# Score and maximum pairs in groups of six, pv halves in threes

## The chip, the cores and the metric

The kernel runs on one core of one Trainium2 chip. The metric is the device time of one execution in microseconds, as the median over runs. The core's engines are named as in the profile: PE is TensorE (PEld its weight loads), DVE is VectorE, ACT is ScalarE, POOL is GpSimd, and SP issues transfers. Each engine works through its own queue in order; semaphores make one engine wait for another.

## The reference

A transformer block with modulation by a condition vector `c`, over 2048 rows of 512: softmax attention with 32 heads of 16, then a gated feed-forward layer of width 1792.

```python
def _A_ref(x, wqkv, wo):
    B, S, D = x.shape
    H = 32; Dh = D // H
    qkv = (lambda x, *d: x.transpose(*d))((x @ wqkv).reshape(B, S, 3, H, Dh), 2, 0, 3, 1, 4)
    q, k, v = qkv[0], qkv[1], qkv[2]
    scale = Dh ** -0.5
    scores = jnp.einsum("bhqd,bhkd->bhqk", q, k) * scale
    p = _softmax(scores, axis=-1)
    o = jnp.einsum("bhqk,bhkd->bhqd", p, v)
    return (lambda x, *d: x.transpose(*d))(o, 0, 2, 1, 3).reshape(B, S, D) @ wo

def _B_ref(x, w_gate, w_up, w_down):
    g = _silu(x @ w_gate)
    u = x @ w_up
    return (g * u) @ w_down
...
h = _layernorm(x, axis=-1) * (1 + ca) + sa
x = x + ga * _A_ref(h, A_wqkv, A_wo)
h = _layernorm(x, axis=-1) * (1 + cb) + sb
x = x + gb * _B_ref(h, B_w_gate, B_w_up, B_w_down)
```

All of it is in float32; where the kernel uses the faster fp32r type, it splits a number into a high and a low part.

## The kernel before

**Stages.** First the normalised rows are projected to q, k and v. Then attention runs. While it runs, the feed-forward layer of the first three of four chunks of 512 rows is worked into it; the last chunk comes behind it.

**Attention.** A unit is one chunk of 512 queries and one group of four heads; there are 32 units of 16 steps, one step for each 128 keys, so n = 512 steps. A step has four scores, one for each head, and two pv halves. Three things run at different places of the sequence:

- `max_one` (L470): a matmul of 128 queries by 512 keys (L479) into one of the banks of the turn `four`, and a maximum over the keys on DVE (L481). It runs LEAD = 21 steps ahead of the scores, because a softmax needs the row maxima before its exps. Four of them belong to each step.
- `max_rows` (L483): once for a unit, when its maxima are complete, the row maxima are reduced (L486), negated (L498), turned into rows by PE (L491 to L493, in a bank from the turn `bank`), copied by ACT (L495) and stored beside q (L497), so that the score matmul subtracts them. It is appended to the list `side`, whose entries are run one after each pair: the turning is the fifth entry.
- `score` (L500): a matmul of 128 keys by 512 queries (L506) into a bank of the turn `bank`, and the exp on ACT into a tile `pt_` (L508). There are PTS = 13 such tiles.
- `pv_step` (L510): one half of 256 queries: four matmuls, one for each head, each onto 32 rows of the unit's own bank 7 (L521). In the profile a half shows as two passes of four. A step's four `pt_` tiles come free with its second half. After the last step of a unit ACT copies the bank out (L525).

A pair (`pair_of`, L903) is one score and one `max_one`. The order of the heads is chosen so that the two matmuls lie on opposite halves of the rows of PE, and the profile shows them side by side.

**The order of PE** is written by hand. `pvs(most, by_halves)` (L914) issues up to `most` pv halves of steps whose scores are all at least four pairs back; with `by_halves` it stops at the end of a unit and owes what is left to the next call. There are two kinds of stretches:

- `plain(steps, tails)` (L936): attention alone. `four` turns over banks 0 to 3, `bank` over banks 4, 5 and 6. It works in windows of WIN = 3 pairs, each followed by one or two pv halves (HALVES = 2, 1, 1, 2). With `tails`, transposes for the feed-forward layer come behind the last windows.
- `filled(places, work)` (L949): eight pairs with feed-forward matmuls between them, then up to six pv halves.

`end_steps` (L930) calls `after(i)` for steps that are done, which issues the loads and stores that have come due and the calls of `max_rows`.

**Where `plain` is called.** Once with 147 steps before any feed-forward work; then for each of the first three chunks with 9 steps, and with 3 steps with tails; with 3 steps ahead of the last two `down` jobs of the first two chunks; with 21 steps between chunks, twice; and with 24 steps (REST) in the third chunk. The calls without tails are nine, with 147, 9, 3, 21, 9, 3, 21, 9 and 24 steps.

Of the kernel before, what the change touches and what calls it, by code (L numbers as in the profile page):

```python
# [39 lines left out]
WIN = 3  # L40
HALVES = (2, 1, 1, 2)
# [60 lines left out]
def block_kernel(ctx, tc, x, wqkv, wo, w_gate, w_up, w_down, c, w_mod, out):  # L102
# [19 lines left out]
    four, bank, single = Turn(0, 1, 2, 3), Turn(4, 5, 6), Turn(7)  # L122
# [387 lines left out]
    def pv_step(i, half):  # L510

        u, kt = divmod(i, 16)
        g = u % NG
        cols = slice(half * HQ, (half + 1) * HQ)
        if kt == 0 and half == 0:
            pv[u] = single("pv")
            o_[u] = pf.tile([P, CW], F32, name="o", tag="o", bufs=2)
        p_ = pts.pop(i) if half else pts[i]
        for h in range(4):
            e0 = (kt * H + 4 * g + h) * (DH + 1)  # L520
            nc.tensor.matmul(pv[u][32 * h:32 * h + 32, cols], v_flat[:, e0:e0 + 32], p_[h][:, cols],  # L521
                             start=(kt == 0 and half == 0), stop=(kt == 15),
                             skip_group_check=half == 1)
        if kt == 15 and half:
            nc.scalar.copy(o_[u], pv[u])  # L525
# [318 lines left out]
    def close_unit(u, i):  # L844

        if u == NU - 1:
            res[u] = out_a(u, nc.scalar)
            return
        res[u] = out_a(u, nc.sync)
        if u + 3 < NU:  # L850
            load_k(u + 3)
            load_q(u + 3)
        i0 = i if u % NG == NG - 1 else i + 2
        at(i0 + 3, lambda: res.__setitem__(u, out_b(u, nc.sync, *res[u])))
        at(i0 + 4, lambda: res.__setitem__(u, out_r(u, nc.sync, *res[u])))
        at(i0 + 5, lambda: out_c(u, nc.gpsimd, nc.gpsimd, *res.pop(u)))
        if u % NG == NG - 1:
            if u // NG:
                at(i + 4, lambda: begin(u // NG))
                at(i + 5, lambda: chunks[u // NG].load_wo())  # L860
            at(i + 7, lambda: chunks[u // NG].load_o(nc.gpsimd))
            at(i + 9, lambda: chunks[u // NG].split_o())
# [37 lines left out]
    done, ended, owed = 0, 0, 0  # L900
    three = Turn(0, 1, 2)

    def pair_of():  # L903
        nonlocal done
        i = done // 4 - 1
        most = 4 * n - 4 * (LEAD - 1)
        score(i + 1, (ORDER if done < most else (0, 1, 2, 3))[done % 4])
        if done < most:
            max_one(done + 4 * (LEAD - 1))
        done += 1  # L910
        if side:
            side.pop(0)()

    def pvs(most, by_halves):  # L914

        nonlocal owed
        if by_halves:
            most, owed = most + owed, 0
        while most and halves and 4 * halves[0][0] + 8 <= done:
            i, half = halves.pop(0)  # L920
            pv_step(i, half)
            most -= 1
            if i % 16 == 15 and half:
                close_unit(i // 16, done // 4 - 1)
                if by_halves:
                    break
        if by_halves and most and halves and 4 * halves[0][0] + 8 <= done:
            owed = most

    def end_steps():  # L930
        nonlocal ended
        while ended < done // 4:
            after(ended - 1)
            ended += 1

    def plain(steps, tails=()):  # L936

        nonlocal four, bank
        assert steps % WIN == 0 and done % 4 == 0
        four, bank = Turn(0, 1, 2, 3), Turn(4, 5, 6)  # L940
        for w in range(4 * steps // WIN):
            for _ in range(WIN):
                pair_of()
            if w >= 4 * steps // WIN - len(tails):
                tails[w - 4 * steps // WIN](four())
            pvs((HALVES[(w - 2) % 4] if done > 8 else 0) + (w == 4 * steps // WIN - 1), True)
            end_steps()

    def filled(places, work):  # L949
# [25 lines left out]
    for ci in range(last):  # L975
        plain(STARTS[ci] - done // 4)
        ch = chunks[ci]
        for t0 in (0, 2):
            work = out_pair(ch, t0, outs, True)
            filled(TWO, work)  # L980
            filled(TWO, work)
        side.append(lambda: scaled(ch))
        plain(NORM)
        plain(WIN, [lambda tp, k=k: ch.turned(tp, k) for k in range(NK)])
        if ci == last - 1:
            plain(REST)
        for _ in range(len(ch.jobs) - (KEEP if ci == last - 1 else 0)):
            job, args = ch.jobs.pop(0)
            if args == (NF // FG - 1, 0):
                plain(WIN)  # L990
            work = job(ch, *args, outs, True)
            for places in (TWO, TWO) if job is gate_up else (DOWN,):
                filled(places, work)
# [73 lines left out]
```

## Time and profile before

| | |
|---|---|
| median of 3 runs | 1879.55 us |
| lowest and highest run | 1879.51 and 1881.34 us |
| span of the profiled execution, first to last instruction | 1875.6 us |
| PE busy in it | 1846.7 us |
| DVE busy in it | 1541.8 us |
| ACT busy in it | 1252.4 us |

The page gives no other time for the profiled execution than its span, so sums are made against the span, and the 3.95 us between span and median are carried along. Engines overlap: their busy times add up to more than the span. A line such as `L506 PE MATMUL bank<-qop,kop` names the line of the kernel, the engine, the operation, and what is written from what. In a listing in order of time the first number is the start and the second the duration, both in us; the part in square brackets is the idle time before it and what ended it. A matmul counts as busy from its start until its last result is written, so that PE looks full when matmuls follow each other without overlapping fully.

### The profile page before, as it was taken

What the parts mean: (1) busy time and instruction counts of PE and PEld (TensorE: products, weight loads), DVE (VectorE), ACT (ScalarE), POOL (GpSimd) and SP (SyncE); (2) the same over time, 40 slices, a digit from 0 to 9 for tenths busy, and PEclk for the clock granted to TensorE, in tenths of its full rate; (3) what the DMA queues carried; (4) which work ended last, traced back from release to release, by engine and by line L of the source; (5) the groups of instructions that cost most, each with busy time, mean ns of one, the idle gap of its engine ahead of it and who ended that gap; (6) DMA issues with size and microseconds to landing.
All of it is one profiled execution on the core that took longest, in us unless ns stands there. A gap on an engine that the chain in (4) does not pass through costs nothing.

```text
span 1875.6 us, 41002 instructions
## 1 busy us (share of the span) xinstructions
PE 1846.7 (98%) x16996; PEld 1160.4 (62%) x16996; DVE 1541.8 (82%) x2558; ACT 1252.4 (67%) x2406; POOL 415.3 (22%) x498
## 2 busy tenths in 40 slices
PE   7999999999999999999999999999999999999999
PEld 5766444444455766666555667666554566667887
DVE  5548999999999888888999888889999988831643
ACT  4221888888887766777777776677878877674211
POOL 3000454456323211111133111111123011030200
PEclk9999999999999999999999999999999999999999
DMA  8855677766843534554454454453643446243642
GB/s 286 292 198 142 174 183 178 201 167 190 211 86 78 145 102 124 144 124 90 107 124 116 108 127 131 121 122 78 159 86 56 108 92 156 86 159 119 249 180 110
DMA packets 78854, 267.62 MB, mean 143 GB/s; under 512 B 17364, under 2 KB 22484, under 8 KB 57988
## 3 DMA queue, kind: packets, MB, share of 16 engines
q1 hardware_dynamic: 59820, 180.10, 33.0%
q0 software_dynamic: 18160, 84.10, 19.0%
q8 instruction: 133, 2.18, 0.5%
q10 hardware_dynamic: 688, 0.80, 0.1%
q14 instruction: 53, 0.43, 0.1%
HBM read 201.85 MB, written 62.13 MB: 141 GB/s over the span
## 4 chain that ended last, share of the span: by engine, by line
PE 95%; DVE 2%; ACT 2%; DMA 0%; issue 0%; SPq 0%; ACTq 0%; DVEq 0%
PE bank L521 26%; PE bank L506 22%; PE bank L719 19%; PE bank L479 10%; PE bank L729 7%; PE bank L209 7%; DVE mx L481 1%; PE bank L762 1%; PE bank L491 1%; PE bank L162 0%; PE bank L703 0%; DMA wm_ab<-in_w_mod 0%; DVE stt L745 0%; PE bank L279 0%; PE bank L493 0%; PE bank L492 0%
## 5 line engine op out<-in xcount | busy, mean ns | idle before, releaser
L481 DVE TENSOR_REDUCE mx<-bank 128x1 f32<-128x512 f32 x2048 | 1286.5, 682 | 119.5 <-PE bank L479 72.4
L479 PE MATMUL bank<-kop,qop 48*128 48x512 f32 x2048 | 748.0, 432 | 3.6 <-DVE mx L481 3.4
L506 PE MATMUL bank<-qop,kop 50*128 50x512 f32 x2048 | 742.1, 427 | 4.6 <-ACT pt__20499 L508 0.5
L506 PEld LDWEIGHTS bank<-qop,kop 50*128 50x128 f32 x2048 | 347.0, 184 | 305.6 <-issue 63.3
L479 PEld LDWEIGHTS bank<-kop,qop 48*128 48x128 f32 x2048 | 343.9, 184 | 30.7 <-DVE mx L481 14.4
L719 PE MATMUL bank<-act,wgu 64*128 64x512 f32 x1872 | 297.9, 392 | 0.0
L719 PEld LDWEIGHTS bank<-act,wgu 64*128 64x128 f32 x1872 | 188.4, 187 | 30.9 <-DVE m L779 0.3
L548 POOL TENSOR_TENSOR on<-o,rb 128x512 f32<-128x512 f32 x31 | 39.7, 1282 | 442.9 <-DMA rb<-d_dr 304.0
L719 PE MATMUL bank<-wd,mid 64*128 64x512 f32 x912 | 136.5, 397 | 0.0
L781 POOL CAST mid<-m 128x512 fp32r<-128x512 f32 x40 | 24.3, 609 | 430.1 <-PE bank L479 165.5
L719 PEld LDWEIGHTS bank<-wd,mid 64*128 64x128 f32 x912 | 93.3, 185 | 12.0 <-issue 0.8
L209 PE MATMUL bank<-hT,wqs 128*128 128x512 f32 x384 | 95.7, 399 | 2.1 <-DVE prt L369 0.8
L209 PEld LDWEIGHTS bank<-hT,wqs 128*128 128x128 f32 x384 | 70.3, 188 | 24.3 <-issue 6.1
L777 DVE SCALAR_TENSOR_TENSOR q<-th,bank 128x512 f32<-128x512 f32 x56 | 37.7, 673 | 57.4 <-ACT th L773 57.2
L773 ACT ACTIVATE th<-bank 128x512 f32<-128x512 f32 x56 | 33.2, 593 | 58.3 <-PE bank L729 57.9
L793 DVE TENSOR_TENSOR x<-bank,x 128x512 f32<-128x512 f32 x84 | 53.8, 684 | 20.4 <-PE bank L506 20.2
L369 DVE TENSOR_TENSOR prt<-bank,prt 128x512 fp32r<-128x512 f32 x32 | 22.0, 688 | 46.5 <-ACT prt L367 46.5
L367 ACT CAST prt<-bank 128x512 fp32r<-128x512 f32 x32 | 18.8, 587 | 60.2 <-PE bank L209 46.9
L779 DVE TENSOR_TENSOR m<-bank,q 128x512 f32<-128x512 f32 x56 | 38.7, 691 | 21.2 <-PE bank L729 19.1
L729 PE MATMUL bank<-wd,mid 128*128 128x512 f32 x216 | 52.1, 394 | 0.4 <-DVE mid L782 0.3
L782 POOL TENSOR_TENSOR mid<-m,mid 128x512 fp32r<-128x512 f32 x40 | 51.6, 1291 | 3.3
L719 PE MATMUL bank<-wgu,act 64*128 64x512 f32 x288 | 47.7, 394 | 0.1
(6282 smaller groups left out, 5155.0 us busy)
## 6 DMA issues: line engine op xcount, KB each, us to landing
wgu<-gu_dr SPq DMA_DIRECT2D x48, 1024.0 KB
wd<-wd_dr SPq DMA_DIRECT2D x28, 1024.0 KB
kop<-kd SPq DMA_DIRECT2D x33, 768.0 KB
kop<-kd POOLq DMA_DIRECT2D x29, 768.0 KB, 8.5
gu_dr<-wgu POOLq DMA_DIRECT2D x14, 1024.0 KB, 14.1
kd<-prt SPq DMA_DIRECT2D x16, 512.0 KB
qd<-prt SPq DMA_DIRECT2D x16, 512.0 KB
kop<-gu_dr SPq DMA_DIRECT2D x8, 1024.0 KB
```

The lines of the kernel that those rows point to most:

```text
L209: nc.tensor.matmul(pt, lhs(a, k), rhs(b, k), start=(n == 0), stop=(n == 3 * nk - 1))
L479: nc.tensor.matmul(pm, qop[u][rows, s, qt * P:(qt + 1) * P], kop[u % 3][rows, s, kc * CW:(kc + 1) * CW], start=True, stop=True)
L481: nc.vector.tensor_reduce(mx[u][:, b, s, qt, kc:kc + 1], pm, op=ALU.max, axis=AX.X)
L506: nc.tensor.matmul(sp, kop[u % 3][rows, h // 2, kt * P:(kt + 1) * P], qop[u][rows, h // 2, :], start=True, stop=True)
L521: nc.tensor.matmul(pv[u][32 * h:32 * h + 32, cols], v_flat[:, e0:e0 + 32], p_[h][:, cols], start=(kt == 0 and half == 0), stop=(kt == 15), ...
L548: mul.tensor_mul(on, o, rb)
L719: nc.tensor.matmul(outs[e], lhs(e, a, k)[rows], rhs(b, k)[rows], start=(ph == 0 and j == 0), stop=(j == z and (ph == 1 or trade is not None)),
L729: nc.tensor.matmul(outs[e], lhs(e, a, k), rhs(b, k), start=(j == 0), stop=(j == z))
L777: nc.vector.scalar_tensor_tensor(q, th, 1.0, outs[0], op0=ALU.add, op1=ALU.mult)
L779: nc.vector.tensor_mul(m32, outs[1], q)
L782: (nc.gpsimd if slow else nc.vector).tensor_sub(mid[:, 1, :], m32, mid[:, 0, :].bitcast(F32))
L793: nc.vector.tensor_add(ch.x2[:, t, :], outs[e], ch.x2[:, t, :])
```

## The change

Only `plain` is changed. Without tails it now works in groups of six pairs, each followed by three pv halves; the number of pairs and halves is the same. With tails it works in windows of three as before.

```diff
         nonlocal four, bank
         assert steps % WIN == 0 and done % 4 == 0
         four, bank = Turn(0, 1, 2, 3), Turn(4, 5, 6)
-        for w in range(4 * steps // WIN):
-            for _ in range(WIN):
+        width = 3 if tails else 6
+        parts = 4 * steps // width
+        for w in range(parts):
+            for _ in range(width):
                 pair_of()
-            if w >= 4 * steps // WIN - len(tails):
-                tails[w - 4 * steps // WIN](four())
-            pvs((HALVES[(w - 2) % 4] if done > 8 else 0) + (w == 4 * steps // WIN - 1), True)
+            if w >= parts - len(tails):
+                tails[w - parts](four())
+            most = HALVES[(w - 2) % 4] if tails else 3
+            pvs((most if done > 8 else 0) + (w == parts - 1), True)
             end_steps()
```

## The prediction

> **What bounds the kernel now.** I read the page first, then busy time by stage, then the order of instructions inside one stage. The page's head:
>
> ```profile
> span 1875.6 us, 41002 instructions
> ...
> PE 1846.7 (98%) x16996; PEld 1160.4 (62%) x16996; DVE 1541.8 (82%) x2558; ACT 1252.4 (67%) x2406; POOL 415.3 (22%) x498
> ...
> PEclk9999999999999999999999999999999999999999
> ```
>
> By these shares PE is the bound. But a matmul that is in flight counts as busy, so I ask each stage. Only the nine calls of `plain` without tails change. Their limits are where L506 has issued 4 scores for each step: 147 steps, 9, 3, 21, 9, 3, 21, 9 and 24, in all 246 steps or 984 pairs. Busy time by window, one window for each call:
>
> ```profile
> core 0: us, PE busy (x) PEld busy (x) DVE busy (x) ACT busy (x) POOL busy (x), PEclk, DMA share, GB/s
> 189.10:547.08 357.98, 357.35 (x3568) 167.31 (x3567) 355.82 (x606) 312.49 (x616) 172.07 (x176) 1.00 0.69 179
> 575.33:599.63 24.30, 23.52 (x227) 10.71 (x223) 23.69 (x45) 19.62 (x39) 7.06 (x20) 1.00 0.39 62
> 886.66:894.05 7.39, 7.24 (x76) 3.27 (x72) 7.30 (x13) 5.97 (x12) 2.57 (x3) 1.00 0.11 37
> 909.30:960.45 51.15, 50.82 (x515) 23.72 (x512) 50.77 (x87) 44.76 (x88) 14.00 (x18) 1.00 0.67 158
> 988.39:1012.65 24.26, 23.51 (x226) 10.70 (x222) 23.68 (x45) 19.62 (x39) 7.04 (x20) 1.00 0.40 59
> 1299.63:1307.03 7.40, 7.28 (x77) 3.27 (x74) 7.33 (x13) 5.99 (x12) 3.30 (x4) 1.00 0.11 37
> 1322.29:1373.66 51.37, 51.12 (x514) 23.97 (x510) 50.68 (x87) 44.77 (x88) 13.98 (x18) 1.00 0.66 155
> 1401.53:1425.84 24.31, 23.52 (x226) 10.70 (x223) 23.71 (x45) 19.60 (x39) 7.04 (x20) 1.00 0.38 59
> 1435.33:1494.29 58.96, 58.69 (x593) 27.57 (x590) 58.06 (x100) 51.23 (x102) 6.81 (x8) 1.00 0.33 67
> sum 607.12, PE 603.05 PEld 281.22 DVE 601.05 ACT 524.04 POOL 233.86; mean PE 67.01 PEld 31.25 DVE 66.78 ACT 58.23 POOL 25.98
> ```
>
> DVE is busy 601.05 of 607.12 us. Six pairs take 357.98 / 98 = 3.65 us in the long call, and six maxima on DVE take 3.6 (below). So DVE bounds these stages now, and anything that only makes PE quicker there can gain 607.12 - 601.05 = 6.1 us at most. What matters is whether six pairs in a row still feed DVE in time.
>
> Six in a row already occur once at the start of each of the eight later calls, because no pv half is ready after the first three pairs. The one at the start of the 24-step call, PE in order of time (score matmuls, then the first matmul of each pv pass; a half is two passes):
>
> ```profile
> 1435.33 0.49 PE L506 MATMUL bank<-qop,kop 50*128 50x512 f32 x1
> ...
> 1435.66 0.39 PE L506 MATMUL bank<-qop,kop 50*128 50x512 f32 x1
> ...
> 1435.90 0.40 PE L506 MATMUL bank<-qop,kop 50*128 50x512 f32 x1
> 1436.51 0.50 PE L506 MATMUL bank<-qop,kop 50*128 50x512 f32 x1 [0.21 <-ACT pt__17219 L508]
> ...
> 1436.99 0.49 PE L506 MATMUL bank<-qop,kop 50*128 50x512 f32 x1
> ...
> 1437.48 0.50 PE L506 MATMUL bank<-qop,kop 50*128 50x512 f32 x1
> ...
> 1437.91 0.40 PE L521 MATMUL bank<-pt__17165,v_flat 128*32 128x256 f32 x1
> ...
> 1438.15 0.38 PE L521 MATMUL bank<-pt__17165,v_flat 128*32 128x256 f32 x1
> ...
> 1438.59 0.38 PE L521 MATMUL bank<-pt__17165,v_flat 128*32 128x256 f32 x1
> ...
> 1438.91 0.50 PE L506 MATMUL bank<-qop,kop 50*128 50x512 f32 x1
> ```
>
> The exps and the maxima of the same stretch:
>
> ```profile
> 1435.86 0.60 ACT L508 ACTIVATE pt__17219<-bank 128x512 f32<-128x512 f32 x1 [0.23 <-PE bank L479]
> 1436.35 0.59 ACT L508 ACTIVATE pt__17224<-bank 128x512 f32<-128x512 f32 x1
> 1436.83 0.60 ACT L508 ACTIVATE pt__17229<-bank 128x512 f32<-128x512 f32 x1
> ```
>
> ```profile
> 1435.89 5.48 DVE L481 TENSOR_REDUCE mx<-bank 128x1 f32<-128x512 f32 x9 [0.43 <-PE bank L479]
> ```
>
> Scores 2 and 3 follow at 0.33 and 0.24 us. The fourth starts at 1436.51, just after exp 1 ends (1435.86 + 0.60), because scores have three banks (4, 5, 6). The fifth and sixth then come one exp apart, 0.49. Nine maxima in 5.48 us, the last lasting about 0.68, are 0.60 each.
>
> **The change part by part.** It adds no instruction; the order on PE changes, and with it the waits.
>
> *What it saves.* Two windows of three, from rows 1438.91 above and here:
>
> ```profile
> 1440.82 0.50 PE L506 MATMUL bank<-qop,kop 50*128 50x512 f32 x1
> ...
> 1442.28 0.50 PE L506 MATMUL bank<-qop,kop 50*128 50x512 f32 x1
> ```
>
> Two halves: 1440.82 - 1438.91 = 1.91; one half: 1.46; together 3.37 for six pairs. Without any wait a group of six needs 0.33 + 4 x 0.24 + 0.32 and then 0.24 + 4 x 0.22 + 0.32, about 3.05. So 0.32 of PE's own time goes, and it was under DVE's 3.6 already: gain nothing, or up to the 6.1 us above. In the Trainium skill, TensorEngine Tiling, Tiling Modes, changing the tiling mode drains TensorE, which speaks for fewer changes; the rows agree (pass to pair 0.32 against pass to pass 0.22), and by that rule alone the change could only gain.
>
> *The wait it adds.* In a group of six the scores 4 to 6 must wait for exps 1 to 3 of the same group; in a window of three the exps ran under the pv halves. By the rows above the first pass starts 1437.91 - 1435.33 = 2.58 after the first score, two halves take 1438.91 - 1437.91 = 1.00 to the next score, and a third adds two passes, 1438.59 - 1438.15 = 0.44 (0.45 by 1.91 - 1.46; I take 0.44). A group is 2.58 + 1.44 = **4.02 us against 3.65**. Behind the waiting load on PE stand maximum 4, pairs 5 and 6 and the pv halves, and DVE waits for the next group's first maximum: 4.02 - 6 x 0.60 = 0.42 idle in each group, and ACT 4.02 - 6 x 0.49 = 1.1. A steady group starts like the row run: by then ACT has long done the previous exps. So I write a call as 2.70 for each group with halves and 0.44 for each half.
>
> - 147 steps: 98 groups (the first without a half), 292 halves: 98 x 2.58 + 97 x 0.12 + 292 x 0.44 = 393.0, less 357.98: +35.0.
> - 21 steps, twice: 14 x 2.70 + 42 x 0.44 = 56.3, less 51.15 and 51.37: +10.0.
> - 24 steps: 16 x 2.70 + 48 x 0.44 = 64.3, less 58.96: +5.4.
> - 3 steps, twice: 2 x 2.70 + 6 x 0.44 = 8.0, less 7.39 and 7.40: +1.3.
> - 9 steps, three times. Here DVE has its own extra work at the start:
>
> ```profile
> 581.69 3.67 DVE L481 TENSOR_REDUCE mx<-bank 128x1 f32<-128x512 f32 x6
> ```
>
> The first twelve pairs are held by DVE, before and after: the sixth maximum of this row starts near 584.7, so twelve pairs last to about 584.9, 9.6 us, either way. Four groups with 13 halves remain: 4 x 2.70 + 13 x 0.44 = 16.5. 9.6 + 16.5 = 26.1 less 24.3: +1.8 each, +5.4.
>
> *Once for each unit of 16 steps:* the row transposes (L491 to L493) take a score bank and PE time inside a group, after its fifth pair:
>
> ```profile
> 298.24 0.39 PE L506 MATMUL bank<-qop,kop 50*128 50x512 f32 x1
> ...
> 298.69 0.39 PE L491 MATMUL bank<-ident,nm 128*16 128x128 f32 x2
> ...
> 299.45 0.50 PE L506 MATMUL bank<-qop,kop 50*128 50x512 f32 x1
> ```
>
> They start 0.45 after the fifth score, when exp 3 has freed their bank, and the sixth score follows 0.76 later than it would. Bounds: 0, and 299.45 - 298.24 - 0.24 = 0.97. I take 0.76, since the place matches. The indices i = 10 mod 16 give 9 + 1 + 1 + 2 = 13 in the calls of 147, 21 and 24 steps, +9.9; one falls in each 9-step call, mostly under DVE's load, at 0.6: +1.8. The copy of the finished unit on ACT stands ahead of the next group's first exp:
>
> ```profile
> 309.55 0.59 ACT L525 COPY o<-bank 128x512 f32<-128x512 f32 x1
> ```
>
> It starts when the last pass ends, about at the next score; that exp would start 0.53 after it anyway (1435.86 - 1435.33). So 0.1 (0 to 0.59), 12 times: +1.2.
>
> *At nothing:* the ring of 13 exp tiles. In 70 of 164 groups the sixth exp needs a tile that the group's own first pv half frees: it starts near 3.2 after the first score in place of 2.9 and ends at 3.8, while its bank is wanted by the next group's third score at 4.02 + 0.57 = 4.6. Eight groups after a unit's end have exps 4 to 6 wait for two halves, but they carry five or six halves, which cover that. No DMA is moved past another; what `after` issues comes at most three pairs later.
>
> **Sum:** 35.0 + 10.0 + 5.4 + 1.3 + 5.4 + 9.9 + 1.8 + 1.2 = 70.0 us on the span of 1875.6: 1945.6. The runs' median stands 3.95 above that span: 1879.55 + 70 = **1950**, 3.7% slower.
>
> **Rivals.**
> 1. *Extras covered:* the row transposes and copies hide, only the group's period counts: 35.0 + 10.0 + 5.4 + 1.3 + 5.4 = 57, 1937. For it: they hide now, under DVE. Against: the path would be PE's, where they lie.
> 2. *Not slower:* the place is the fourth score's bank. If scores 4 to 6 did not wait in a steady group, PE would need 3.05, DVE stays the bound and gets its gaps back: 1879.55 - 6.1 = 1873.5. It decides from a group of 3.65, a sixth score at most 1.78 after the first instead of 2.15. Against it: the rows show 2.15.
> 3. *The tile ring binds:* the sixth exp's lateness of 0.3 passes to the next group in those 70 groups, +21: 1971. Against: 0.8 of cover.
> 4. *The clock falls:* PE now pauses in every group. Six passes at double 0.22 add 1.3 to 164 groups, +213: 2163. Against: the granted clock is 1.00 in all windows, also where these runs of six stand. The Trainium skill, TensorE: Matmul & The Clock Gate, in the section on psum-queue depth-cycling, says that pauses of PE while it cycles PSUM banks can make the clock oscillate; the trace has not shown it.
> 5. *Nothing happens:* owed halves bring the old order back: 1879.5. Against: followed through the loops, 138 of 164 groups get three or two halves behind six pairs.
>
> **How the numbers follow.** Forecast 0.72, then 0.15, 0.04, 0.06, 0.02, 0.01. The forecast's own range: 1937 with no extras, 1963 with all upper bounds (13 x 0.21 + 12 x 0.49, and 0.45 for each of 436 halves). The whole range takes that and a little below: 1932 to 1963. A measurement tells about 0.2% from no change: faster 0.04, same 0.01, slower 0.95.
>
> **What would show it.** Right: in the long call scores 4 to 6 start 0.05 after an exp's end and 0.49 apart, the first pass 2.58 after the group's first score, six pairs take 4.0 us, DVE falls from 99% to about 90% there, and the call lasts 393 to 402 us. Filled stages stay as they are. Wrong: six pairs in 3.65 with DVE at 99% (rival 2), exps that start after a pv half with scores behind them (3), a clock under 1.00 (4).

## The result, and the profile after

The changed kernel takes 1961.2 us (median of 4 runs, 1958.46 to 1962.59) against 1879.8 us for the kernel before: a ratio of 1.0431, 95% interval 1.0416 to 1.0445, or 81 us more. The forecast was 1950 with a range to 1963: the direction held, and the size came out 11 us short, near the upper end of the range. The profiled execution's span grew by 85.2 us. The page's head after:

```profile
span 1960.8 us, 41097 instructions
...
PE 1895.5 (97%) x16996; PEld 1174.2 (60%) x16996; DVE 1551.5 (79%) x2558; ACT 1251.9 (64%) x2406; POOL 415.0 (21%) x498
...
PEclk9999999999999999999999999999999999999999
```

Each engine has as many instructions as before (the 95 more in the total are semaphore instructions, 89 of them on ACT) and about the work that it had. The windows of the nine changed calls (busy time of PE, PEld, DVE, ACT and POOL, then the granted clock, the DMA share and GB/s):

```profile
189.54:598.98 409.44, 385.74 (x3568) 175.43 (x3568) 363.76 (x607) 312.44 (x616) 171.81 (x176) 0.99 0.60 157
626.92:654.22 27.30, 25.43 (x227) 11.47 (x223) 24.20 (x45) 19.75 (x39) 7.02 (x20) 1.00 0.38 60
941.24:949.29 8.05, 7.69 (x77) 3.45 (x73) 7.75 (x13) 6.09 (x12) 3.20 (x4) 1.00 0.10 34
964.42:1022.32 57.90, 54.45 (x516) 24.78 (x512) 51.96 (x87) 44.65 (x88) 13.95 (x18) 1.00 0.60 142
1050.23:1079.13 28.90, 27.02 (x226) 11.95 (x223) 24.24 (x45) 19.75 (x39) 7.00 (x20) 0.94 0.34 58
1366.18:1374.21 8.03, 7.72 (x76) 3.46 (x72) 7.79 (x13) 6.09 (x12) 3.76 (x4) 1.00 0.10 34
1389.33:1448.98 59.65, 56.28 (x514) 25.63 (x511) 51.95 (x87) 44.66 (x88) 13.93 (x18) 0.97 0.60 139
1476.86:1504.16 27.30, 25.43 (x226) 11.46 (x222) 24.24 (x45) 19.76 (x39) 7.02 (x20) 1.00 0.37 61
1513.66:1579.91 66.25, 62.48 (x593) 28.62 (x590) 59.47 (x100) 51.06 (x102) 6.81 (x8) 1.00 0.31 66
sum 692.82, PE 652.24 PEld 296.25 DVE 615.36 ACT 524.26 POOL 234.49; mean PE 72.47 PEld 32.92 DVE 68.37 ACT 58.25 POOL 26.05
```

692.82 - 607.12 = 85.7 us against the span's 85.2: all of the loss lies in these calls and none outside. DVE's share in the long call falls from 99% to 363.76 / 409.44 = 89%. A steady group on PE (its six scores and the next group's first):

```profile
299.30 0.50 PE L506 MATMUL bank<-qop,kop 50*128 50x512 f32 x1
299.63 0.39 PE L506 MATMUL bank<-qop,kop 50*128 50x512 f32 x1
299.87 0.40 PE L506 MATMUL bank<-qop,kop 50*128 50x512 f32 x1
300.48 0.50 PE L506 MATMUL bank<-qop,kop 50*128 50x512 f32 x1 [0.21 <-ACT pt__2627 L508]
...
300.97 0.50 PE L506 MATMUL bank<-qop,kop 50*128 50x512 f32 x1
...
301.46 0.49 PE L506 MATMUL bank<-qop,kop 50*128 50x512 f32 x1
...
303.31 0.50 PE L506 MATMUL bank<-qop,kop 50*128 50x512 f32 x1
```

and its maxima on DVE, then those of the next group:

```profile
299.86 3.68 DVE L481 TENSOR_REDUCE mx<-bank 128x1 f32<-128x512 f32 x6 [0.34 <-PE bank L479]
...
303.88 3.68 DVE L481 TENSOR_REDUCE mx<-bank 128x1 f32<-128x512 f32 x6 [0.18 <-PE bank L506]
```

The fourth score waits for the group's first exp, the fifth and sixth come 0.49 apart, the sixth starts 2.16 us after the first, and 303.31 - 299.30 = 4.01. DVE has an idle piece in front of each six maxima (0.34 and 0.18, the latter behind a small reciprocal). In the kernel before, 27 maxima in a row show none:

```profile
229.39 16.22 DVE L481 TENSOR_REDUCE mx<-bank 128x1 f32<-128x512 f32 x27
```

Two things stand out beside that. The first is a unit's end, where the group before had only one half. ACT there, in order of time:

```profile
418.13 0.60 ACT L508 ACTIVATE pt__3956<-bank 128x512 f32<-128x512 f32 x1 [0.22 <-PE bank L521]
418.62 0.58 ACT L525 COPY o<-bank 128x512 f32<-128x512 f32 x1
419.09 0.61 ACT L508 ACTIVATE pt__3973<-bank 128x512 f32<-128x512 f32 x1
```

The score of the exp at 419.09 had started at 417.98. The exp comes 1.11 us after it and not 0.53: ahead of it stood the sixth exp of the short group, late because of its tile, and then the copy. So the group's fourth score starts 1.77 us after its first in place of 1.18, and the group lasts 5.48 us. Where the copy stands behind a group with three halves, no late exp is ahead of it: there the fourth score starts at 1.32 and the group lasts 4.17 us (328.31 to 332.48), only 0.15 more than a steady one.

The second is the clock. At another such place the same kind of group lasts 7.16 us. Windows of its first 3.3 us, of the next 3.41, and of the whole group:

```profile
284.08:287.40 3.32, 2.78 (x20) 1.18 (x20) 3.32 (x6) 2.55 (x5) 2.94 (x4) 0.99 0.92 162
287.40:290.81 3.41, 3.41 (x36) 1.70 (x35) 1.35 (x3) 1.57 (x3) 2.77 (x4) 0.50 1.14 321
284.08:291.24 7.16, 6.62 (x56) 2.90 (x53) 4.67 (x8) 4.13 (x8) 5.70 (x7) 0.76 1.05 240
```

For 3.41 us the granted clock is 0.50, and the pv halves of that group run in it at half speed. The trace has five such stretches in the changed calls, at 195.2, 287.4, 553.6, 1058.8 and 1403.5, each of 3.41 us. The trace of before has none in these calls; other runs of that kernel, with mean clocks down to 0.997, may have had some. Three of the five (287.4, 553.6, 1403.5) stand in groups like this one, at a unit's end. The one at 195.2 comes at the end of the twelve pairs in a row with which the first call begins, and the one at 1058.8 in the second group of a 9-step call, where the pairs wait for DVE. What PE had in the 3.41 us before these two, and in the first 3.41 us of the group at 417.98, which no such stretch follows:

```profile
191.79:195.20 3.41, 3.41 (x16) 1.57 (x14) 3.41 (x7) 3.41 (x9) 1.68 (x3) 1.00 0.83 180
1055.39:1058.80 3.41, 3.29 (x15) 1.64 (x15) 3.41 (x7) 2.55 (x7) 2.40 (x12) 1.00 0.00 0
417.98:421.39 3.41, 2.87 (x20) 1.20 (x20) 3.41 (x7) 2.56 (x5) 3.03 (x4) 1.00 0.88 124
```

The page's clock line shows 9 in every slice, because a slice is 49 us long; the stretches appear only in narrow windows, and in the mean clock of 0.995.

### The profile page after: what moved, and what is told of

Read it like the earlier page. It is cut to its first block, busy times and chain, and to the rows that moved or that the text cites. A ratio compares the mean times of both kernels' runs of the same rounds, so it can differ in the third digit from the quotient of the medians.

```text
span 1960.8 us, 41097 instructions
## 1 busy us (share of the span) xinstructions
PE 1895.5 (97%) x16996; PEld 1174.2 (60%) x16996; DVE 1551.5 (79%) x2558; ACT 1251.9 (64%) x2406; POOL 415.0 (21%) x498
## 4 chain that ended last, share of the span: by engine, by line
PE 87%; ACT 6%; DVE 2%; DMA 2%; POOL 1%; issue 1%; SPq 0%; ACTq 0%; POOLq 0%; DVEq 0%
PE bank L521 24%; PE bank L506 22%; PE bank L719 18%; PE bank L729 7%; PE bank L479 7%; PE bank L209 6%; DVE mx L481 1%; PE bank L762 1%; PE bank L491 1%; DMA rb<-d_dr 1%; ACT o L525 0%; PE bank L162 0%; PE bank L279 0%; DMA wm_ab<-in_w_mod 0%; PE bank L703 0%
## 5 line engine op out<-in xcount | busy, mean ns | idle before, releaser
L506 PE MATMUL bank<-qop,kop 50*128 50x512 f32 x2048 | 803.0, 439 | 40.0 <-ACT pt__20499 L508 0.5
L479 PE MATMUL bank<-kop,qop 48*128 48x512 f32 x2048 | 799.0, 441 | 3.7 <-DVE mx L481 1.9
L506 PEld LDWEIGHTS bank<-qop,kop 50*128 50x128 f32 x2048 | 352.1, 184 | 400.9 <-issue 64.1
L479 PEld LDWEIGHTS bank<-kop,qop 48*128 48x128 f32 x2048 | 349.1, 184 | 31.3 <-DVE mx L481 16.7
L209 PE MATMUL bank<-wqs,hT 128*128 128x512 f32 x192 | 47.5, 397 | 0.0
```

Source lines behind the costliest of these rows:

```text
L209: nc.tensor.matmul(pt, lhs(a, k), rhs(b, k), start=(n == 0), stop=(n == 3 * nk - 1))
L479: nc.tensor.matmul(pm, qop[u][rows, s, qt * P:(qt + 1) * P], kop[u % 3][rows, s, kc * CW:(kc + 1) * CW], start=True, stop=True)
L506: nc.tensor.matmul(sp, kop[u % 3][rows, h // 2, kt * P:(kt + 1) * P], qop[u][rows, h // 2, :], start=True, stop=True)
```

## The experiments

Before each stands what was expected of it. The first four were run once each, beside 1878.93 us for the kernel before; the others are medians of four to ten runs, beside 1879.0 us or, where it is said, 1878.25 us.

**DVE's part taken down, in both orders.** Maxima over half the keys, exps at a sixteenth of their scale. Such a kernel leaves out half of each maximum, so it does not compute the reference's softmax; it has the same instructions in the same order:

```diff
-        nc.vector.tensor_reduce(mx[u][:, b, s, qt, kc:kc + 1], pm, op=ALU.max, axis=AX.X)
+        nc.vector.tensor_reduce(mx[u][:, b, s, qt, kc:kc + 1], pm[:, 0:CW // 2], op=ALU.max, axis=AX.X)
-        nc.scalar.activation(p_, sp, AF.Exp, scale=SCALE)
+        nc.scalar.activation(p_, sp, AF.Exp, scale=SCALE / 16)
```

> The order of before (windows of three), but each maximum on DVE is taken over 256 of the 512 keys, and the exp gets a sixteenth of its scale so that it stays finite; the matmuls are the same. Theory (DVE bounds the windows of three): six pairs fall from 3.65 us towards PE's own 3.37, the 147-step call from 358 to 330 to 340 us, the span from 1876 to about 1835 to 1850. Rival (PE or the exps bound them already): the call stays at 355 to 358 and the time within 5 us of before.

Measured: 1862.91 us, the 147-step call 357.1. That call began with 13.6 us at half clock, so a window of 320 us behind it is the better measure. First this run, then the kernel before:

```profile
220.00:540.00 320.00, 319.00 (x3260) 146.19 (x3260) 198.07 (x551) 283.90 (x561) 156.07 (x163) 1.00 0.68 178
```

```profile
220.00:540.00 320.00, 319.81 (x3209) 150.07 (x3208) 317.88 (x543) 278.65 (x550) 157.63 (x164) 1.00 0.69 180
```

DVE is busy 62% in place of 99%, and yet only 1.5% more of its instructions (551 against 543) fit into the window. The theory expected 5 to 8%, and both its call (330 to 340) and its time were missed. So DVE was the bound in the windows of three, but another limit lay 1.5% under it: where two windows with one half follow each other, the third score already waits for an exp, and such a window takes 1.70 us in both kernels, not PE's own 1.46. So PE's own 3.37 us for six pairs, which the forecast set beside DVE's 3.6, could not be reached either.

> The same shortening of DVE's maximum in groups of six (256 of 512 keys, exp at a sixteenth of its scale). Theory (a group's length comes from scores 4 to 6 waiting for exps 1 to 3, not from DVE): the group stays at 4.02 us, the 147-step call at 400 to 410, the time within 8 us of 1961. Rival (the maximum's banks or DVE bind in the group): the group falls below 3.8 and the time below 1925.

Measured: 1953.27 us, and the long call:

```profile
185.98:594.64 408.66, 384.94 (x3569) 174.78 (x3568) 234.59 (x605) 312.44 (x616) 171.86 (x176) 0.99 0.60 158
```

DVE's busy time there falls from 364 to 235 us, the call stays at 409 and the steady groups at 4.02. DVE does not bind in groups of six.

**The score banks.** The same with four banks for scores and three for maxima, in the calls without tails:

```diff
         width = 3 if tails else 6
+        if not tails:
+            four, bank = Turn(0, 1, 2), Turn(3, 4, 5, 6)
```

> As the run with the shortened maximum in groups of six, and in the calls without tails scores turn over four banks (3 to 6) and maxima over three (0 to 2). Theory (the number of score banks sets the wait): score 5 waits for exp 1 and score 6 for exp 2, so score 6 starts 1.68 us after the first in place of 2.16, the group lasts 3.55 in place of 4.02, the time is about 1884. Rival (the row of six itself, or the pv halves behind it, cost the time): the group stays at 4.0 and the time near 1960.

Measured: 1885.38 us. A group's scores, and the next group's first:

```profile
281.53 0.50 PE L506 MATMUL bank<-qop,kop 50*128 50x512 f32 x1
281.87 0.62 PE L506 MATMUL bank<-qop,kop 50*128 50x512 f32 x2
...
282.33 0.39 PE L506 MATMUL bank<-qop,kop 50*128 50x512 f32 x1
282.91 0.79 PE L506 MATMUL bank<-qop,kop 50*128 50x512 f32 x2
...
285.10 0.49 PE L506 MATMUL bank<-qop,kop 50*128 50x512 f32 x1
```

285.10 - 281.53 = 3.57, where 3.55 was expected and three banks give 4.02. One bank more moves the wait from the fourth score to the fifth and takes 68 us off the time of the run before (1953.27). That is the cause by itself: the same six pairs and three halves in a row, with other banks. About 6 us over the kernel before are left, single run against single run.

With the full maximum, the same bank edit on the changed kernel:

> Groups of six with scores on four banks (3 to 6) and maxima on three (0 to 2), with the full maximum on DVE. Theory: now maximum 6 waits for reduce 3 (0.56 + 2 x 0.60 + 0.68 + 0.05 = 2.49 after the group's start), the group lasts 2.49 + 0.43 + 1.44 = 4.36 us and the span grows to about 2010 to 2020. Rival (only the score banks matter): DVE's 3.6 for a group and about 1890.

Measured: 2008.65 us. The maxima of a group, and the next group's first:

```profile
269.14 0.73 PE L479 MATMUL bank<-kop,qop 48*128 48x512 f32 x2
269.71 0.40 PE L479 MATMUL bank<-kop,qop 48*128 48x512 f32 x1
...
270.46 0.50 PE L479 MATMUL bank<-kop,qop 48*128 48x512 f32 x1
...
271.06 0.50 PE L479 MATMUL bank<-kop,qop 48*128 48x512 f32 x1
271.65 0.49 PE L479 MATMUL bank<-kop,qop 48*128 48x512 f32 x1
...
273.51 0.49 PE L479 MATMUL bank<-kop,qop 48*128 48x512 f32 x1
```

The sixth maximum starts 271.65 - 269.14 = 2.51 after the first (expected 2.49) and the group lasts 4.37 (4.36). With DVE at 0.60 for each maximum, a bank taken from it costs more than the scores gain. Neither of the two divisions of the seven banks tried here (one holds the pv of the unit) keeps six in a row free of waits; others were not tried.

**One half put back into the middle.**

```diff
-            for _ in range(width):
+            for r in range(width):
                 pair_of()
+                if not tails and r == 2:
+                    pvs(1 if done > 8 else 0, True)
...
-            most = HALVES[(w - 2) % 4] if tails else 3
+            most = HALVES[(w - 2) % 4] if tails else 2
```

> Groups of six as in the change, but one of the three pv halves stands behind the third pair and two behind the sixth. Theory (only the missing halves between pair 3 and pair 4 cost time): the exps run under the middle half again, six pairs take DVE's 3.65 us, the time is that of before, 1876 to 1884. Rival (the cost lies in the unit ends or in the number of halves of a group): most of the 80 us stays, over 1920.

Measured: 1883.46 us, ratio 1.0026 (1.0016 to 1.0035). One pv half behind the third pair takes nearly all of the loss away (77 us); a steady group is 3.59 us, DVE's 6 x 0.60:

```profile
303.18:306.77 3.59, 3.59 (x40) 1.62 (x36) 3.03 (x7) 3.05 (x6) 3.44 (x3) 1.00 0.45 144
```

**More work for PE in its waits.** The matmuls of scores 4 and 5 are issued twice:

```diff
-            for _ in range(width):
-                pair_of()
+            for r in range(width):
+                pair_of(r in (3, 4) and not tails)
...
-        nc.tensor.matmul(sp, kop[u % 3][rows, h // 2, kt * P:(kt + 1) * P], qop[u][rows, h // 2, :],
-                         start=True, stop=True)
+        for _ in range(2 if twice else 1):
+            nc.tensor.matmul(sp, kop[u % 3][rows, h // 2, kt * P:(kt + 1) * P], qop[u][rows, h // 2, :],
+                             start=True, stop=True)
```

> The change, with the score matmuls of pairs 4 and 5 of each group issued twice into the same bank (same result). Theory (PE waits there, 0.25 us in each): the group stays at 4.02, and where the clock fell to half after a group with little PE work it falls less often: 1950 to 1962. Rival (PE's own work sets the group): 2 x 0.235 us more in 164 groups, about 2035.

Measured: 1956.57 us (1956.25 to 1958.97), ratio 1.0415 (1.0397 to 1.0432). A group, and the long call (the row with x2 holds the second issue of score 4 and the first of score 5):

```profile
314.66 0.49 PE L507 MATMUL bank<-qop,kop 50*128 50x512 f32 x1
...
315.84 0.50 PE L507 MATMUL bank<-qop,kop 50*128 50x512 f32 x1 [0.22 <-ACT pt__2925 L509]
...
316.18 0.64 PE L507 MATMUL bank<-qop,kop 50*128 50x512 f32 x2
...
318.69 0.50 PE L507 MATMUL bank<-qop,kop 50*128 50x512 f32 x1
```

```profile
187.02:592.05 405.03, 382.26 (x3765) 194.33 (x3764) 364.03 (x607) 313.52 (x616) 172.12 (x176) 1.00 0.61 159
```

318.69 - 314.66 = 4.03: 328 matmuls more, and no steady group is longer; those with the row transposes last 4.95 in place of 4.88. PE really waits there. Of the five stretches at half clock only one is left, at 1051.6 in a 9-step call, and the mean clocks of the four runs are 0.999 to 1.000, against 0.995 to 0.997 in the changed kernel's. The long call, now at a clock of 1.00, takes 405.0 in place of 409.4; for the whole time the intervals of the two ratios overlap. So more work on PE, in groups of the same length, keeps most of the stretches away. Whether it is the amount of work or the length of the pauses that counts was not separated.

**The unit's copy on DVE**, except for the last unit:

```diff
-            nc.scalar.copy(o_[u], pv[u])
+            (nc.scalar.copy if u == NU - 1 else nc.vector.tensor_copy)(o_[u], pv[u])
```

> The change, with the copy of a finished unit (L525) on DVE in place of ACT, except for the last unit. Theory (behind a group with one half the copy delays ACT's next exps by 0.6 us, and that quiet stretch is what lets the clock fall): the groups of five or six halves shrink by 0.6, the 7.2 us groups vanish, 1948 to 1956. Rival (the short group alone makes the quiet stretch): only about 5 us less at most, half-clock stretches stay as many, 1955 to 1962.

Measured: 1958.36 us (1953.79 to 1961.69), ratio 1.0419 (1.0400 to 1.0438); the theory fell in both parts. The exps are early again, but the copy now delays the maxima. The last two maxima and the sixth score of the group that lasted 5.48 us:

```profile
420.79 0.49 PE L479 MATMUL bank<-kop,qop 48*128 48x512 f32 x1
420.79 0.50 PE L506 MATMUL bank<-qop,kop 50*128 50x512 f32 x1
421.39 0.49 PE L479 MATMUL bank<-kop,qop 48*128 48x512 f32 x1
```

The sixth maximum starts 0.6 behind its score, since DVE has to release its bank, and the group grows from 5.48 to 5.66. And the stretches at half clock at 288.1 and 554.3 are still there, beside one of 10.24 us at 192.5 in the first call: 17.1 us at half clock, as much as in the changed kernel. So the copy on ACT is not needed for them. That the short group alone makes them is not shown, since here the copy delays the same groups on DVE.

**The change in parts:** six in a row in the first call only, then in the eight later calls only.

```diff
-        width = 3 if tails else 6
+        three_wide = tails or done
+        width = 3 if three_wide else 6
...
-            most = HALVES[(w - 2) % 4] if tails else 3
+            most = HALVES[(w - 2) % 4] if three_wide else 3
```

> Groups of six only in the call of 147 steps; the eight later calls keep windows of three. Theory (the cost is paid in each call where the groups stand and nothing of it is given back later): that call takes 405 to 410 us as in the change, against 358, and the time is 1879 + 47 to 51, 1926 to 1931. Rival (part of the loss is made up later, by loads or GpSimd work that then finish earlier relative to the rest): under 1920.

> The complement: windows of three in the call of 147 steps, groups of six in the eight later calls. Theory (costs add): the rest of the change's 81 us, 1908 to 1914. Rival (the calls depend on each other): the two parts together miss the change's 81 us by over 8.

Measured: 1926.38 us, ratio 1.0249 (1.0231 to 1.0268), and 1915.46 us, ratio 1.0197 (1.0181 to 1.0214), against 1878.25. The second misses its band of 1908 to 1914 by 1.5 us. 48.1 + 37.2 = 85.3 against the change's 81: the costs add, within the few us by which runs with such stretches differ, and nothing is made up later. The first call of the first run has the same order of instructions as in the changed kernel, but its stretches stand at 192.6, 284.7 and 417.8: the third in the group at a unit's end that went without one there. So which place gets a stretch differs from one execution to the next.

## Why the prediction came out as it did

**The bound before:** DVE, as said, but with less room than said. The forecast set PE's own 3.37 us beside DVE's 3.6 and left out that windows of three also wait for exps. The second limit is 1.5% under DVE. This does not touch the sum, which used measured lengths of the calls; it makes the second rival (not slower) weaker than it was priced.

**The added wait:** right, in mechanism and size. 4.02 us for a group was read from a run of six that was already in the trace of before, and the steady group is 4.01 to 4.03. With the maxima halved the call did not move. Banks were named as the place, and one more bank moved the wait as worked out (3.57 against 3.55).

**The sum by calls,** forecast with the unit terms and measured: long call +42.7 and 409.44 - 357.98 = +51.5; the two of 21 steps +11.7 and +15.0; 24 steps +7.0 and +7.3; 3 steps +1.3 and +1.3; 9 steps +7.2 and +10.6. So 70 against 85.7 in the profiled execution: the time lies inside the range because the range was wide enough for it, not because these parts were foreseen. Three terms were mis-sized:

- *The clock*, priced as a rival for every group (+213, chance 0.02), came in five places. A stretch of 3.41 us at half speed costs about 1.7: the long groups at unit ends take 7.16 with it and 5.48 without, and calls of equal length that differ by one stretch differ by 28.90 - 27.30 = 1.6 and 59.65 - 57.90 = 1.75. 5 x 1.7 = 8.5 us, over half of what was missing. The Trainium skill (TensorE: Matmul & The Clock Gate, the section on psum-queue depth-cycling) says that pauses of PE between groups of matmuls while it cycles PSUM banks can make the clock swing between half and full. This trace agrees only in part: the clock fell five times for 3.41 us, and no steady group, which also pauses and cycles banks, had a stretch.
- *The unit's copy*, taken at 0.1 us. Behind a group with one half it stands after a late sixth exp, and the group with five halves takes 5.48 where 2.70 + 5 x 0.44 = 4.90 was counted: 0.6 for each of eight such groups, 4.8, where five copies at 0.1 were counted in them: 4.3 more than forecast. A copy without a late exp ahead of it costs 0.15 (above), so the step that failed is that the tile ring was put at nothing. Its late exp was covered against the third score of a group that begins 4.02 us after; behind a group with one half the next begins after 3.17, its third score is 0.23 late (0.80 after the first, not 0.57), and the copy and exp 1 stand behind the late exp on ACT. The copies were also counted 12 times where the nine calls hold 17.
- *The row transposes*, taken at 0.76:

```profile
269.65 0.49 PE L506 MATMUL bank<-qop,kop 50*128 50x512 f32 x1
270.24 0.39 PE L491 MATMUL bank<-ident,nm 128*16 128x128 f32 x2
...
271.00 0.49 PE L506 MATMUL bank<-qop,kop 50*128 50x512 f32 x1
272.85 0.50 PE L506 MATMUL bank<-qop,kop 50*128 50x512 f32 x1
```

They start 0.59 behind the fifth score, not 0.45, and the group, whose first score was at 267.97, lasts 4.88: 0.86 more than 4.02. 13 x 0.1 = 1.3.

Together 14.1 of the 15.7 that were missing in the span. Of the rest, 0.8 lies in the first two groups of the first call, 9.08 us with a stretch of about 1.7 where 2.58 + 4.02 = 6.60 were counted. The median moved by 4 us less than the span of the profiled run. In the changed kernel's runs the time is 1.8 us above the span. If it was so before too, the 3.95 us that the forecast carried along are 1.8 of this kind and 2.1 by which the profiled execution was quicker than the median; on the changed side the profiled run, 1962.59, is 1.4 slower than its median. Of the four runs two have a mean clock of 0.995 (1962.0 and 1962.6 us) and two of 0.997 (1958.5 and 1960.5).

**Rivals.** Extras covered: no, each unit pays. Not slower: no, the sixth score starts 2.16 after the first. The tile ring: not in steady groups, but at unit ends, as above. The clock: in five places, not in every group. Nothing happens: no.

## What to carry to other kernels

A row of n matmuls into b banks ran freely here only for the first b; from then on it went at the pace of the engine that empties the banks, and whatever was queued behind the row was late: the sixth score started 2.16 us after the first with three banks and 1.67 with four, one exp of 0.49 less. Work that needs none of these banks belongs between the matmuls that do; one pv half in the middle was worth 77 us here. Before a change of order is costed, look in the trace for a place where the new order already occurs by chance: its length is the price. No version tried here that computes the reference is faster than the kernel before, and the run with the shortened maxima suggests why there is little to find in these calls with windows of three: with DVE out of the way, the next limit is 1.5% off.

## What had not been expected of the hardware

Five stretches at half clock came in a kernel whose PE the page calls 97% busy. Each lasts 3.41 us. Three stand in the long group behind a group with one half; the other two follow twelve pairs in a row without a half, and pairs that wait for DVE. With one half back in the middle two came, at 192.7 and 994.8, both within 6 us of the start of a call, and the kernel with windows of three and shortened maxima began its first call with 13.6 us at half clock. No steady group of six pairs and three halves had one in the trace. How little work on PE it takes was not measured, and it cannot be read from the counts: 15, 16 and 20 matmuls in 3.41 us came before a stretch, and 20 at 417.98 did not bring one.
